# Re-forming the first token half of a fused attention and MLP kernel: two PSUM tiles for the second affine, row sums on ScalarE, a quarter of the value sort on GpSimd

## The chip, the core and the metric

The kernel runs on one core of a Trainium2 chip, from one launch. A core has five engines with a queue each: TensorE (PE in the profile, with its weight loads shown as PEld), VectorE (DVE), ScalarE (ACT), GpSimd (POOL) and SyncE (SP). Each works through its own instructions in the order of its queue, and they wait for each other by semaphores. The metric is the device time of one execution in microseconds (us); lower is better.

## The reference

Two stages, in float32, with batch 4, 8 heads, 768 positions, head size 64, 8 blocks of 96 positions, and a model width of 512:

```
P = sort_net                                  # (4, 8, 8, 8)
5 times: P = exp(P - max); P /= row sum; P /= column sum
k_sorted, v_sorted = P mixed over the 8 blocks of k and of v
attn = softmax(q_block . k_sorted_block^T / 8) . v_sorted_block   # inside a block of 96
x    = attn, heads side by side               # (4, 768, 512)
a1   = alpha1 * x + beta1
u    = x + lam * (w_tok @ a1)                 # w_tok is 768 x 768, over positions
a2   = alpha2 * u + beta2
out  = u + lam * (relu(a2 @ w_ch1) @ w_ch2)   # 512 -> 2048 -> 512
```

## The kernel before

The four batches run one after the other. The MLP of a batch is done in two halves of 384 positions. For a half, 16 hidden tiles of 128 units are made from the transposed input `a2T` (four matmuls of 128x384 each, `h_unit`; the page calls the output `h_ps`), and three tiles of 128 positions of output are made from them (16 matmuls of 128x512 each, `ch_unit`, `ch_ps`). All else, such as the attention of the next batch, the token product and the loads, is hung between these by the tables `put` and `run`: a key (batch, half, "h" or "c", number) says after which unit a piece is issued. There is no planner that moves an instruction. The class `Engine` keeps every instruction in the order in which the Python code issues it, so the order written by hand is the order of each queue. All compute instructions therefore show one source line, L65, and are told apart by their tiles.

Nothing can be hung between units before the first `a2T` of batch 0 exists. That head of the kernel, some 42 us, is what is touched here. Its steps are:

1. Five normalisations of `P` on VectorE and ScalarE, beside transposes of the queries on TensorE and `warm` matmuls on zeros, whose outputs nobody reads. The table `beside` holds what goes beside each.
2. `mix_keys` and `mix_values` spread `P` into the matrices `bigK` and `bigV`; `k_turn` and `k_copy` mix and transpose the keys of batch 0; `v_sort` re-orders the loaded values `v8` into `VD` (four instructions of 16 head columns: 128 partitions x 768 elements of float16, read with a stride of 64 elements), and `v_mix` makes the sorted values `Vs` from it, eight columns at a time. `score` gives the softmax numerators `et`, one group of heads and one half of the blocks per call.
3. `pv_first(g)` gives the attention output `x` for two heads (128 columns), in positions that are permuted so that all 128 partitions are used. `permute` copies `w_tok` into the same order (`wp`), `prep_wtok` transposes it on TensorE and copies it into `w_tokT`. "Half" 0 is the first 384 rows of `w_tok`.
4. The first token half. The columns of `u` come transposed straight from TensorE. For each of four groups of 128 columns, `first_tok` makes the token product in one PSUM tile (`tok_ps`, six matmuls), and begins a second tile (`turn_ps`) with the transposed `x` and a rank-one term, row sums of `w_tok` times `beta1 * lam`. ScalarE scales the product by `lam * alpha1` into `tok16`, and `first_turn` adds that to the second tile by a matmul with the identity. ScalarE's `affine` then reads the second tile and writes `a2T`. The row sums themselves are six matmuls against a column of ones (`row_sums`, `rr_ps`), and the per-column parameters are transposed by `prep_ab2`.

What sets the order around the change, in words of the code: lines 748 to 808 are the hand-written order of steps 2 to 4; lines 880 to 888 start the hidden tiles of the first half, with the last `first_turn` between them; lines 824 to 834 hang the second half of `w_tok` (`prep_wtok(ks, 1, ...)`), the rest of `a1` and the first output sums (`first_back`) between the first hidden tiles. PSUM tiles come from two pools: `psa` with two tiles of two banks, `psb` with four tiles of one bank. A tile is handed out again, in turn, once its last reader is done. GpSimd's queue issues the large loads (line 115 on, 149 to 155, 169 to 173, 299, 810); such an issue waits when the load that last used the same semaphore has not landed. The values `v8` are the third load.

```
    v_sort(0, act.copy)
    v_sort(1, copy)
    score(0, 0, 0, psa)
...
    for ci in range(2):
        for m in range(3):
            h_part(0, 0, m, [ci])
    first_turn(3, t3, act)
```

Of the kernel before, what the change touches and what calls it, by code (L numbers as in the profile page):

```python
# [7 lines left out]
FT = mybir.dt.float32  # L8
F16 = mybir.dt.float16
BF = mybir.dt.bfloat16  # L10
AF = mybir.ActivationFunctionType
ALU = mybir.AluOpType
# [4 lines left out]
def kernel(  # L17
# [25 lines left out]
    C = H * D  # L43
# [45 lines left out]
    def psb(shape, dtype, name):  # L89
        return pools["psB"].tile(shape, dtype, name=name, tag="psB")  # L90

    def const(shape, dtype, name):
        return wts.tile(shape, dtype, name=name, tag=name)
# [54 lines left out]
    for half in range(2):  # L148
# [7 lines left out]
        if half == 0:  # L156
# [2 lines left out]
                KT0[:].rearrange("p g i (th t) -> p (g i th) t", th=2)[:, :, HB:64].bitcast(FT), 0.0  # L159
            )  # L160

    W1p = const([128, CT, HID], BF, "W1p")
    W2p = const([128, HT, C], BF, "W2p")
    w1v = moe_w_ch1.rearrange("(ci p) n -> p ci n", p=128)
# [4 lines left out]
    pool.dma_start(alphaB[:], moe_alpha1.partition_broadcast(128))  # L169
    pool.dma_start(betaB[:], moe_beta1.partition_broadcast(128))  # L170
    pool.dma_start(lamB[:], moe_lam.partition_broadcast(128))
    for g in range(4):
        pool.dma_start(W1p[:, :, g * 512:(g + 1) * 512], w1v[:, :, g * 512:(g + 1) * 512])
    brow = att.tile([1, C], F16, name="brow", tag="uT", bufs=2)
    rrow = att.tile([1, 384], F16, name="rrow", tag="uT", bufs=2)
    ones16 = const([128, 1], F16, "ones16")
    pool.memset(ones16[:], 1.0)
    pool.tensor_tensor(brow[:], bet1[:], lam1[:], ALU.mult)

    vscr = dram.tile([B, H * NB, BLK, D], F16, name="vscr", tag="vscr")  # L180
# [41 lines left out]
    def warm(n, ps=psa):  # L222
        fill(ps([128, 512], FT, "warm_ps")[:], n)
# [27 lines left out]
            ps[half].rearrange("p (t r) -> p r t", t=6),  # L251
        )

    def v_sort(n, eng):
        eng(
            VD[:, n * 16:(n + 1) * 16, 0:HB],
            v8[:, :, n * 16:(n + 1) * 16].rearrange("p t d -> p d t"),
        )

    rsum = const([BH, NB], FT, "rsum")  # L260
    csum = const([BH, NB], FT, "csum")
# [6 lines left out]
    def q_out(g):  # L268
        for half in range(2):
            q_copy(0, g, qps[g], half, act.copy)  # L270
# [3 lines left out]
        1: [lambda: q_first(1), lambda: warm(2), lambda: warm(3)],  # L274
        2: [lambda: q_first(2), lambda: warm(3)],
        3: [lambda: q_out(0), lambda: q_first(3)],
        4: [lambda: q_out(1), lambda: q_out(2), lambda: q_out(3), lambda: warm(5)],
    }
    warm(12)
    for it in range(5):  # L280
# [89 lines left out]
    def k_turn(b, g, ps):  # L370
        return turn_slab(k8, lambda r, g: bigK[b][r, g, :], g, "k_ps", ps)
# [61 lines left out]
    def pv_first(g):  # L433
        if g == 0:
            x_of[0] = moep.tile([128, 8, C], F16, name="x128", tag="x128", bufs=2)
            a1_of[0] = moep.tile([128, 8, C], F16, name="a1", tag="a1", bufs=1)
        ps = psa([128, 2, 512], FT, "x_ps")[:, :, 0:480].rearrange("p a (k d) -> p a k d", d=80)
        for i in range(NB):
            for h2 in range(2):
                et = ets[(0, g, i // 4)][:].rearrange("p a i t -> p (a i t)")  # L440
                lo = (4 * h2 + i % 4) * BLK
                w = min(128, 8 * BLK - lo)
                val = Vs[0][:, (2 * g + h2) * NB + i, 0:D + 1]
                if i < 6:
                    pe.matmul(ps[0:w, h2, i, 0:D + 1], et[:, lo:lo + w], val, start=True, stop=True)
                else:
                    for a in range(3):
                        pe.matmul(
                            ps[96:128, h2, 3 * (i - 6) + a, 0:D + 1], et[:, lo + a * 32:lo + (a + 1) * 32], val,
                            start=True, stop=True,  # L450
                        )
        rc = att.tile([128, 2, 6], FT, name="rc", tag="rc", bufs=3)
        dve.reciprocal(rc[:], ps[:, :, :, D])
        dve.tensor_tensor(
            x_of[0][:, 0:NT, g * 128:(g + 1) * 128].rearrange("p k (a d) -> p k a d", a=2),
            ps[:, :, :, 0:D].rearrange("p a k d -> p k a d"),
            rc[:].rearrange("p a k -> p k a").unsqueeze(3).to_broadcast([128, NT, 2, D]), ALU.mult,
        )
# [100 lines left out]
    w_tokT = const([128, NT, S], F16, "w_tokT")  # L559
    wp_of = {}  # L560

    def permute(half, eng):
        wp = wp_of[half] = (moep, att)[half].tile(
            [128, 3, NT, 128], F16, name="wp", tag=("u16", "raw")[half], bufs=(1, 2)[half]
        )
        src = wt16[half]
        eng(wp[:, :, :, 0:96], src[:, :, 0:TAIL].rearrange("p m (k c) -> p m k c", c=96))
        eng(wp[:, :, :, 96:128], src[:, :, TAIL:S].rearrange("p m (k c) -> p m k c", c=32))

    def prep_wtok(ks, half, ps, eng):  # L570
        pst = ps([128, 384], F16, "wtok_ps")
        for m in range(3):
            pe.transpose(pst[:, m * 128:(m + 1) * 128], wp_of[half][:, m, ks, :], ident16[:])
        eng(w_tokT[:, ks, half * 384:(half + 1) * 384], pst[:])

    ab2col = const([128, 4 * CT], FT, "ab2col")

    def prep_ab2(ps):
        tps = ps([128, 4 * CT], FT, "ab2_ps")
        pe.transpose(tps[:], ab2[:], ident16f[:])  # L580
        act.copy(ab2col[:], tps[:])
        dve.tensor_tensor(
            ab2col[:, 3 * CT:4 * CT], ab2col[:, 2 * CT:3 * CT], ab2col[:, 3 * CT:4 * CT], ALU.mult
        )

    def row_sums(ps):
        ps = ps([1, 384], FT, "rr_ps")
        for ks in range(NT):
            pe.matmul(ps[:], ones16[:], w_tokT[:, ks, 0:384], start=(ks == 0), stop=(ks == NT - 1))
        act.copy(rrow[:], ps[:])  # L590

    u_of = {}
# [5 lines left out]
    def affine(b, hf, ci, src, eng):  # L598
        dst = a2T_of[b][hf][:, ci, :]
        if eng is act:  # L600
            act.activation(
                dst, src, AF.Identity, bias=ab2col[:, CT + ci:CT + ci + 1], scale=ab2col[:, ci:ci + 1],
            )
        else:
            dve.tensor_scalar(
                dst, src, ab2col[:, ci:ci + 1], ab2col[:, CT + ci:CT + ci + 1], op0=ALU.mult, op1=ALU.add,
            )
# [5 lines left out]
            u_of[b] += [t_[:, kt, :] for kt in range(3)]  # L613
        a2T_of[b] = [moep.tile([128, CT, 384], BF, name=f"a2T_{hf}", tag="a2T", bufs=3) for hf in range(2)]

    def first_tok(g):
        c = slice(g * 128, (g + 1) * 128)
        tps, ups = (psb([128, 384], FT, n)[:] for n in ("tok_ps", "turn_ps"))
        for ks in range(NT):
            pe.matmul(  # L620
                tps, x_of[0][:, ks, c], w_tokT[:, ks, 0:384], start=(ks == 0), stop=(ks == NT - 1),
            )
        for m in range(3):
            pe.matmul(
                ups[:, m * 128:(m + 1) * 128], x_of[0][:, m, c], ident16[:],
                start=(m == 0), stop=True, skip_group_check=True,
            )
        pe.matmul(ups, brow[:, c], rrow[:], start=False, stop=True, skip_group_check=True)
        act.activation(tok16[:, g, :], tps, AF.Copy, scale=ab2col[:, 3 * CT + g:3 * CT + g + 1])
        return ups  # L630

    def first_turn(g, ups, eng):
        pe.matmul(ups, ident16[:], tok16[:, g, :], start=False, stop=True, skip_group_check=True)
        affine(0, 0, g, ups, eng)

    def first_back(m, ps):
        ps = ps([128, C], FT, "back_ps")
# [107 lines left out]
    def wtok(ks, eng):  # L745
        prep_wtok(ks, 0, psb, eng)

    mix_keys(0, psb)
    warm(4)
    kp0 = k_turn(0, 0, psb)  # L750
    kp1 = k_turn(0, 1, psb)
    k_copy(0, 0, kp0, 0, copy)
    k_copy(0, 0, kp0, 1, act.copy)
    warm(1)
    kp2 = k_turn(0, 2, psb)
    k_copy(0, 1, kp1, 0, copy)
    k_copy(0, 1, kp1, 1, act.copy)
    kp3 = k_turn(0, 3, psb)
    k_copy(0, 2, kp2, 0, copy)
    k_copy(0, 2, kp2, 1, act.copy)  # L760
    mix_values(0, psb)
    k_copy(0, 3, kp3, 0, copy)
    k_copy(0, 3, kp3, 1, act.copy)
    v_sort(0, act.copy)
    v_sort(1, copy)
    score(0, 0, 0, psa)
    score(0, 0, 1, psa)
    warm(3, psb)
    v_mix(0, 0, psb, copy)
    v_mix(0, 1, psb, copy)  # L770
    v_sort(2, copy)
    score(0, 1, 0, psa)
    v_mix(0, 2, psb, copy)
    v_mix(0, 3, psb, act.copy)
    v_sort(3, act.copy)
    score(0, 1, 1, psa)
    v_mix(0, 4, psb, copy)
    v_mix(0, 5, psb, copy)
# [2 lines left out]
    v_mix(0, 7, psb, copy)  # L781
    dve.tensor_copy(Vs[0][:, :, D:GRP], mgap[:].unsqueeze(2).to_broadcast([128, H * NB, GRP - D]))
    score(0, 2, 1, psa)
    permute(0, copy)
    moe_start(0)
    warm(1, psb)
    pv_first(0)
    wtok(0, act.copy)
    wtok(1, act.copy)
    wtok(2, act.copy)  # L790
    score(0, 3, 0, psa)
    pv_first(1)
    wtok(3, act.copy)
    wtok(4, act.copy)
    wtok(5, act.copy)
    score(0, 3, 1, psa)
    permute(1, copy)
    row_sums(psb)
    prep_ab2(psb)
    t0 = first_tok(0)  # L800
    pv_first(2)
    first_turn(0, t0, act)
    t1 = first_tok(1)
    pv_first(3)
    first_turn(1, t1, act)
    t2 = first_tok(2)
    first_turn(2, t2, act)
    t3 = first_tok(3)

    load_kv(1)  # L810
    load_q(1)
# [5 lines left out]
    def put(b, hf, kind, n, *todo):  # L817
        at.setdefault((b, hf, kind, n), []).extend(todo)
# [5 lines left out]
    for kt in range(3, NT):  # L824
        put(0, 0, "h", 4 + kt, lambda kt=kt: moe_tok(0, kt, psb))
    for ks in range(NT):
        put(0, 0, "h", ks, lambda ks=ks: prep_wtok(ks, 1, psb, (dve.tensor_copy, act.copy)[ks % 2]))
    for n in range(1, B):
        put(max(n - 2, 0), n > 1, *(("h", 10), ("c", 9))[n > 1], lambda n=n: mix_matrix(n))
    put(0, 0, "h", 9, lambda: moe_cross(0, 1))  # L830
# [46 lines left out]
        put(b, 0, "h", 4, lambda b=b: moe_cross(b, 1))  # L877
        put(b, 0, "h", 13, lambda b=b: moe_affine(b, 1))

    for ci in range(2):  # L880
        for m in range(3):
            h_part(0, 0, m, [ci])
    first_turn(3, t3, act)
    for m in range(3):
        h_part(0, 0, m, [2])
    for m in range(3):
        h_part(0, 0, m, [3])
        run(0, 0, "h", m)
# [41 lines left out]
```

## Time and profile before

| What | Value |
|---|---|
| Median of 9 runs | 274.42 us (272.89 to 275.54) |
| Profiled execution, its own time | 276.2 us |
| Its span, from first to last instruction | 274.4 us |
| Mean granted TensorE clock | 0.994 of full speed |
| Busy: PE, DVE, ACT, POOL | 95%, 62%, 43%, 35% of the span |
| First hidden matmul that completes a tile | starts at 41.90 us |

The page's first part gives the busy time of each engine. The second cuts the span in 40 slices of 6.9 us and shows tenths of busy time in each. The chain of waits follows the last instruction back to whatever released it, step by step, and so shows the work that set the end; each line is a start, a length and a piece of work, "x6" being six instructions. A timeline lists one engine's instructions with the idle time before them, and a table of groups gives the mean length of one instruction. In the profile a matmul's length includes its latency; the distance from one start to the next is what a row of matmuls costs.

### The profile page before, as it was taken

The numbers are of one execution on the slowest core, as the hardware profiler recorded it, in microseconds if no ns is written. First come the engines' busy times: TensorE is split into PE (matmuls) and PEld (weight loads), VectorE is DVE, ScalarE is ACT, GpSimd is POOL, SyncE is SP. The second block draws the span as 40 slices with busy tenths as digits, with TensorE's granted clock in tenths as the row PEclk, the third lists the DMA queues.
The fourth block names the chain that finished last, engine by engine and source line by source line (L and its number), as shares of the span: only waits on it lengthen the run. The fifth ranks groups of instructions, "written<-read, shape, count | busy, mean of one in ns | idle before, by whom it ended". The sixth has DMA issues, their size and how long they took to land.

```text
span 274.4 us, 5380 instructions
## 1 busy us (share of the span) xinstructions
PE 261.3 (95%) x2173; PEld 140.5 (51%) x2173; DVE 169.8 (62%) x351; ACT 117.1 (43%) x219; POOL 96.4 (35%) x104
## 2 busy tenths in 40 slices
PE   7888999999999999999999969999999999999993
PEld 3455655455556444554565424554465445545552
DVE  5778427896558978576778725586689756121032
ACT  2578648234787002453674002444674004604600
POOL 8647202701472094403570814402300746122000
PEclk9999999999999999999999997999999999999999
DMA  6999999997989942249399942149300223012012
GB/s 100 194 205 201 206 208 214 174 122 178 128 168 174 141 116 78 59 115 155 79 188 161 113 124 67 38 118 118 102 13 2 73 61 76 22 38 76 0 41 76
DMA packets 67372, 31.04 MB, mean 113 GB/s; under 512 B 56642, under 2 KB 63058, under 8 KB 67348
## 3 DMA queue, kind: packets, MB, share of 16 engines
q0 software_dynamic: 26352, 15.34, 40.4%
q1 hardware_dynamic: 40900, 15.30, 30.6%
q8 instruction: 17, 0.28, 0.4%
q14 instruction: 7, 0.06, 0.1%
q10 hardware_dynamic: 96, 0.07, 0.1%
HBM read 32.79 MB, written 8.65 MB: 151 GB/s over the span
## 4 chain that ended last, share of the span: by engine, by line
PE 85%; DVE 5%; DMA 4%; issue 2%; ACT 1%; SPq 1%; POOL 0%; DVEq 0%; POOLq 0%
PE h_ps L65 30%; PE ch_ps L65 28%; PE tok_ps L65 12%; PE x_ps L65 3%; DMA q<-in_q_dram 3%; PE sc_ps L65 3%; DVE ost L65 2%; PE kmix_ps L65 1%; PE mix_ps L65 1%; PE warm_ps L65 1%; DVE x L65 1%; DVE a L65 1%; SPq L670 1%; PE turn_ps L65 1%; PE v_ps L65 1%
## 5 line engine op out<-in xcount | busy, mean ns | idle before, releaser
L65 PE MATMUL h_ps<-a2T,W1p 128*128 128x384 bf16 x512 | 96.8, 327 | 2.7 <-DVE a2T L65 2.4
L65 ACT ACTIVATE hTa<-h_ps 128x384 bf16<-128x384 f32 x96 | 47.0, 492 | 95.5 <-PE h_ps L65 95.3
L65 PE MATMUL ch_ps<-W2p,hTa 128*128 128x512 bf16 (+1 forms) x300 | 68.5, 371 | 0.0
L65 POOL TENSOR_TENSOR ost<-ost,u 128x512 f32<-128x512 f32 x21 | 26.6, 1266 | 116.5 <-DVE ost L65 110.4
L65 PEld LDWEIGHTS <-W1p 128*128 128x128 bf16 x512 | 47.5, 99 | 35.2 <-issue 4.8
L65 PEld LDWEIGHTS <-hTa 128*128 128x128 bf16 x300 | 28.4, 98 | 29.0
L65 DVE TENSOR_TENSOR ost<-ch_ps,lamB 128x512 f32<-128x512 f32 (+1 forms) x25 | 16.7, 669 | 37.8 <-PE ch_ps L65 34.6
L65 POOL TENSOR_TENSOR u<-toktmp,x 128x512 f32<-128x512 f32 x18 | 29.2, 1635 | 6.7 <-DVE toktmp L65 6.7
L65 PE MATMUL tok_ps<-a,w_tokT 128*128 128x512 f16 x126 | 31.0, 391 | 0.0
L65 ACT ACTIVATE et<-sc_ps 96x768 f16<-96x768 f32 (+1 forms) x32 | 25.6, 812 | 10.9 <-PE sc_ps L65 10.9
L65 PE MATMUL ch_ps<-W2p,hTb 128*128 128x512 bf16 (+1 forms) x100 | 24.8, 370 | 0.0
L65 DVE TENSOR_TENSOR toktmp<-tok_ps,lamB 128x512 f32<-128x512 f32 x21 | 14.4, 687 | 11.9 <-PE tok_ps L65 10.5
L65 PEld LDWEIGHTS <-w_tokT 128*128 128x128 f16 x126 | 12.5, 100 | 14.9 <-issue 1.7
L65 DVE TENSOR_TENSOR u<-toktmp,x 128x512 f16<-128x512 f32 (+1 forms) x24 | 18.9, 799 | 0.7
L65 ACT ACTIVATE hTb<-h_ps 128x384 bf16<-128x384 f32 x32 | 15.7, 490 | 8.0 <-PE h_ps L65 7.6
L65 POOL DMA_DIRECT2D qn<-in_q_dram x18 | 16.0, 924 | 4.6 <-DMA raw<-in_v_dram 4.6
L65 DVE CAST kT<-kmix_ps 64x512 f16<-64x512 f32 x20 | 14.3, 713 | 4.5 <-PE kmix_ps L65 3.0
L65 DVE TENSOR_TENSOR x<-x_ps,rcb 96x512 f16<-96x512 f32 x24 | 16.5, 687 | 0.8
L65 DVE TENSOR_SCALAR a2T<-uT,ab2col 128x384 bf16<-128x384 f16 x28 | 10.5, 440 | 9.5 <-DMA uT<-u 9.5
L65 PE MATMUL x_ps<-Vs,et 96*128 96x65 f16 (+4 forms) x288 | 14.4, 195 | 1.4 <-DVE x L65 1.0
L65 PEld LDWEIGHTS <-et 96*128 96x128 f16 (+4 forms) x288 | 12.4, 100 | 6.3 <-DVE x L65 2.2
L65 ACT CAST kT<-kmix_ps 64x512 f16<-64x512 f32 x16 | 11.5, 716 | 9.8 <-PE kmix_ps L65 9.6
(113 smaller groups left out, 238.1 us busy)
## 6 DMA issues: line engine op xcount, KB each, us to landing
out_dram<-ost SPq DMA_DIRECT2D x23, 192.0 KB, 2.2
raw<-in_v_dram POOLq DMA_DIRECT2D x6, 384.0 KB, 8.0
raw<-in_k_dram POOLq DMA_DIRECT2D x6, 384.0 KB, 10.0
qn<-in_q_dram POOLq DMA_DIRECT2D x18, 128.0 KB, 10.2
vscr<-mixed SPq DMA_DIRECT2D x6, 384.0 KB, 3.6
Vs<-vscr SPq DMA_DIRECT2D x3, 768.0 KB, 7.7
W1p<-in_moe_w_ch_dram POOLq DMA_DIRECT2D x4, 512.0 KB, 13.1
W2p<-in_moe_w_ch_dram POOLq DMA_DIRECT2D x4, 512.0 KB, 17.3
```

The costliest lines, as they stand in the source:

```text
L65: ins = getattr(self.eng, name)(*args, **kwargs)
L670: nc.sync.dma_start_transpose(uT[:, :, m * 128:(m + 1) * 128], u16_of[b][:, 3 * hf + m, :],)
```

## The change

- `first_mm` and `first_turn` replace `first_tok` and the old `first_turn`. The token product stays in its own PSUM tile. The second tile holds the transposed `x` and the rank-one term; ScalarE applies scale and bias to it and writes `z` in float32. VectorE's `first_finish` then forms `a2T = product * (alpha2 * lam * alpha1) + z`. The four matmuls with the identity that added `tok16` are gone; ScalarE still writes `tok16`, which `first_back` needs. `ab2col` gets four more columns for the new factor (`prep_scales`).
- `row_sums`: ScalarE passes over `w_tok` three times with `accum_out` (`row_sum(m)`, output thrown into the still unused tile `a1`), and three small transposes on TensorE turn the sums into a row.
- `v_sort(3)` runs on GpSimd, ahead of the loads of `W1p`; `v_sort(0)` goes from ScalarE to VectorE and `v_sort(2)` from VectorE to ScalarE.
- `mix_values`, `prep_ab2` and `prep_scales` are issued earlier, `permute(0)` is cut in two parts, five of the six `prep_wtok` copies of half 0 go from ScalarE to VectorE, `pv_first(2)` is issued ahead of the token products, the last group's transposes and product (`first_turn(3)`, `first_mm(3)`) stand between the hidden matmuls of `ci` 0 and 1, and the `prep_wtok` of half 1 takes its PSUM tiles from `psa` instead of `psb`.

```diff
+    v_sort(3, pool.tensor_copy)
     for g in range(4):
         pool.dma_start(W1p[:, :, g * 512:(g + 1) * 512], w1v[:, :, g * 512:(g + 1) * 512])
...
-    ones16 = const([128, 1], F16, "ones16")
-    pool.memset(ones16[:], 1.0)
...
+    def row_sum(m):
+        if m == 0:
+            a1_of[0] = moep.tile([128, 8, C], F16, name="a1", tag="a1", bufs=1)
+        act.activation(a1_of[0][:].rearrange("p k c -> p (k c)")[:, 0:S], wt16[0][:, m, :], AF.Copy, accum_out=rcol[:, m:m + 1])
...
     def row_sums(ps):
-        ps = ps([1, 384], FT, "rr_ps")
-        for ks in range(NT):
-            pe.matmul(ps[:], ones16[:], w_tokT[:, ks, 0:384], start=(ks == 0), stop=(ks == NT - 1))
+        rc16 = const([128, 3], F16, "rc16")
+        act.copy(rc16[:], rcol[:])
+        ps = ps([1, 384], F16, "rr_ps")
+        for m in range(3):
+            pe.transpose(ps[:, m * 128:(m + 1) * 128], rc16[:, m:m + 1], ident16[:])
         act.copy(rrow[:], ps[:])
...
+    def first_finish(g):
+        dve.scalar_tensor_tensor(
+            a2T_of[0][0][:, g, :], tps_of[g], ab2col[:, 4 * CT + g:4 * CT + g + 1], z_of[0][:, g, :],
+            op0=ALU.mult, op1=ALU.add,
+        )
+        if g == 3:
+            tok_copy(g)
...
-    def first_turn(g, ups, eng):
-        pe.matmul(ups, ident16[:], tok16[:, g, :], start=False, stop=True, skip_group_check=True)
-        affine(0, 0, g, ups, eng)
...
+        if g == 0:
+            z_of[0] = moep.tile([128, CT, 384], FT, name="z", tag="u32", bufs=3)
+        act.activation(
+            z_of[0][:, g, :], ups, AF.Identity, bias=ab2col[:, CT + g:CT + g + 1], scale=ab2col[:, g:g + 1],
+        )
+        if g < 3:
+            first_finish(g)
...
     mix_keys(0, psb)
     warm(4)
+    mix_values(0, psb)
+    prep_scales()
...
-    mix_values(0, psb)
+    v_sort(0, copy)
+    score(0, 0, 0, psa)
     k_copy(0, 3, kp3, 0, copy)
     k_copy(0, 3, kp3, 1, act.copy)
-    v_sort(0, act.copy)
+    score(0, 0, 1, psa)
     v_sort(1, copy)
...
-    v_sort(2, copy)
+    v_sort(2, act.copy)
...
-    permute(0, copy)
+    row_sum(0)
+    permute(0, copy, 0, 3)
...
-    wtok(0, act.copy)
+    score(0, 3, 0, psa)
+    wtok(0, copy)
     wtok(1, act.copy)
-    wtok(2, act.copy)
-    score(0, 3, 0, psa)
+    wtok(2, copy)
+    permute(0, copy, 3, 6)
+    row_sum(1)
+    row_sum(2)
     pv_first(1)
-    wtok(3, act.copy)
-    wtok(4, act.copy)
-    wtok(5, act.copy)
+    wtok(3, copy)
+    wtok(4, copy)
+    wtok(5, copy)
+    permute(1, copy, 0, 6)
     score(0, 3, 1, psa)
-    permute(1, copy)
+    pv_first(2)
     row_sums(psb)
-    prep_ab2(psb)
-    t0 = first_tok(0)
-    pv_first(2)
-    first_turn(0, t0, act)
-    t1 = first_tok(1)
+    first_mm(0, psb)
+    first_turn(0, psb)
+    first_mm(1, psb)
     pv_first(3)
-    first_turn(1, t1, act)
-    t2 = first_tok(2)
-    first_turn(2, t2, act)
-    t3 = first_tok(3)
+    first_turn(1, psb)
+    first_mm(2, psb)
+    first_turn(2, psa)
...
-        put(0, 0, "h", ks, lambda ks=ks: prep_wtok(ks, 1, psb, (dve.tensor_copy, act.copy)[ks % 2]))
+        put(0, 0, "h", ks, lambda ks=ks: prep_wtok(ks, 1, psa, (dve.tensor_copy, act.copy)[ks % 2]))
...
-    for ci in range(2):
+    for m in range(3):
+        h_part(0, 0, m, [0])
+    first_turn(3, psa)
+    first_mm(3, psa)
+    for ci in (1, 2):
         for m in range(3):
             h_part(0, 0, m, [ci])
-    first_turn(3, t3, act)
-    for m in range(3):
-        h_part(0, 0, m, [2])
```

## The prediction

> **What bounds the kernel now.** First the page: who is busy, and is the clock granted?
>
> ```profile
> PE 261.3 (95%) x2173; PEld 140.5 (51%) x2173; DVE 169.8 (62%) x351; ACT 117.1 (43%) x219; POOL 96.4 (35%) x104
> ...
> PE   7888999999999999999999969999999999999993
> ...
> PEclk9999999999999999999999997999999999999999
> ```
>
> TensorE is full except in the first four slices (0 to 27 us) and in slice 24. So after the head an engine other than TensorE costs nothing unless it makes TensorE wait, and time taken out of the head reaches the end. Next the chain of waits, cut to the head:
>
> ```profile
> 17.42 1.53 ACT vd L65
> ...
> 25.15 1.33 DVE wp L65 x2
> ...
> 29.94 1.06 PE rr_ps L65 x6
> 31.01 0.16 PE ab_ps L65
> ...
> 33.63 0.27 PE turn_ps L65
> ...
> 36.26 0.27 PE turn_ps L65
> ...
> 37.54 0.59 ACT tok L65
> 38.13 0.04 issue
> 38.17 0.32 PE turn_ps L65
> ...
> 40.98 0.18 PE turn_ps L65
> 41.16 0.02 issue
> 41.18 0.68 ACT a2T L65
> 41.86 0.04 issue
> 41.90 0.34 PE h_ps L65
> ```
>
> Up to 25 us the head alternates between TensorE and copies of the value sort. From 30 us it is TensorE's own list, in which the row sums, the parameter transpose, the four adding matmuls and two waits on ScalarE stand.
>
> **Token stage (before: 29.9 to 41.9 us).** Row sums: 1.06 us leave; three transposes come, 0.06 us apart as the `wtok_ps` ones are, with latency 0.2. Gain 0.85. The parameter transpose (0.16) goes to 11 us in the place of one warm matmul (0.21 from start to start): gain 0.15, no cost. The four adding matmuls cost from start to start 0.17, 0.17, 0.57 (0.40 of it the wait for `tok` at 38.1) and 0.16; after the fourth, TensorE stands 0.43 for `a2T` (next matmul due at 41.47, start 41.90). Together 1.5. In the new order the last `a2T` needs the fourth product, which lies six hidden matmuls (6 x 0.163 = 1.0) ahead of its first reader: latency 0.2 and one VectorE instruction. That one has no row. Nearest is `toktmp` (PSUM and SBUF in, 512 elements, 0.69), so 0.55 for 384; bounds 0.45 and 0.7. It fits either way. `z` on ScalarE costs what `a2T` did there (0.67). I count 1.4 of the 1.5, for the transposes' own latencies.
>
> **Middle (25.2 to 31.1 us).** `pv_first(2)` (0.96) moves ahead of the products, so it is neither gain nor loss. VectorE takes five `wtok` copies (0.35 each, 1.8), ScalarE loses five of 0.48 and gets three row sums. No row has an accumulator; a float16 copy of 384 takes 0.48 and an exponential of 768 takes 0.83: I take 0.85, bounds 0.8 and 1.2. At 0.85 they end at 29.4, before the last scores need ScalarE at 29.8; at 1.2 the chain of row sum, transpose and `rrow` copy is late for the first rank-one matmul by 0.3. VectorE now paces this stretch: normalising `x`, 1.22 each for four; `permute` in pieces, 0.6 and 0.3 twice, then 1.4; the copies. Laid end to end, TensorE waits some 0.6 in place of today's 0.3 at 26.2 and the time of the row sums: the stretch from the first `x_ps` to the first product stays 5.9 to 6.0 us although 1.0 us of TensorE work left and 0.96 came. Cost 0.1.
>
> **First stretch (12 to 25.2 us).** `mix_values` now stands before the keys: three VectorE instructions of 0.22 and two of 0.16 come ahead of the first key copy, which ends at 15.8, not 15.24; the third key turn waits for that PSUM tile. The scores start at 17.3, not 17.08. The 0.5 us of "issue" inside the key turns I leave in place. Then the values, which landed at 17.22. Quarter 0 on VectorE: 17.3 to 18.1 (on ScalarE it ended at 18.94). Quarter 1 follows a key copy, 18.45 to 19.25 if nothing blocks it. Quarter 2 on ScalarE ends at 20.95, behind two exponentials; quarter 3 is GpSimd's.
>
> The price of that one: GpSimd's only copy row (256 elements, 0.42) gives 1.25 for 768; the same strided read takes ScalarE 1.51 against 0.83 unstrided, so up to 2.5. [...] I take 1.9; alone it would be done long before it is read (22.8), and costs nothing.
>
> [...] Here VectorE and GpSimd collide:
>
> ```profile
> 64.35 1.62 DVE L65 TENSOR_SCALAR a2T<-uT,ab2col 128x384 bf16<-128x384 f16 x2
> ```
> ```profile
> 64.30 1.27 POOL L65 TENSOR_TENSOR ost<-ost,u 128x512 f32<-128x512 f32 x1 [11.27 <-DVE ost L65]
> ```
> ```profile
> L65 PE MATMUL h_ps<-a2T,W1p x9: 326/326/337, 72.8 to 74.9; 128*128 128x384 bf16 x9
> L65 DVE TENSOR_SCALAR a2T<-uT,ab2col x4: 366/368/1330, 64.1 to 65.9; 128x384 bf16<-128x384 f16 x4
> ```
>
> Three of the four take 0.37; the one that began just after GpSimd's instruction took 1.33 and ended 0.1 after it. Instructions of VectorE that read PSUM show no such growth. [...] So I expect the lock. [...]
>
> The two sums for the first `x_ps`, before 25.21. Without the lock: `v_mix` 4 waits for quarter 2 (20.95), the 0.5 us "issue" gap, the last copies of `Vs` end at 24.2, `x_ps` at 24.35: gain 0.85. With it: `v_mix` 2 at 20.65, 4 at 21.8, gap, last copy 25.05, `x_ps` at 25.1: gain 0.1.
>
> GpSimd's sort also holds back the first `W1p` issue from 17.5 to 20.1. Five earlier loads are still under way then (they land up to 26.7), the queue doesn't run dry at its 205 GB/s, and `W1p` lands at 29, needed at 36.5.
>
> **The sum.** With the lock: 0.1 + 0.85 + 0.15 + 1.4 - 0.1 = 2.4 us: the first completing hidden matmul goes from 41.90 to 39.5. The `prep_wtok` change takes away a 0.25 wait of TensorE for `hTa`, yet gains nothing: VectorE's row of two copies and four `a1` pairs (42.43 to 47.56) ends when the next token product (47.35) reads it, and two `psa` tiles make TensorE wait on it earlier. That row starts 2.4 sooner too. Then TensorE is full, and the shift stays. What doesn't move is the load queue: at 205 GB/s the last queries of batch 1 land at 59.5 now and then. They are read at 64.4, afterwards 62.0: still hidden, and uncovered only past a gain of 4.9. The `uT` transposes come at 54.0 instead of 56.4, more under those loads; their reader on VectorE has no TensorE work behind it until 70. The profiled execution took 276.2, 1.8 more than its span and 1.8 above the median, so I subtract from the median: 274.42 - 2.4 = **272.0 us**.
>
> **The rivals.**
> - No lock, or a sort of 1.2 us: x_ps at 24.35, the gain is 3.1 to 3.2: 271.3. [...]
> - VectorE becomes the bound of the middle: its list from 25 to 32 us holds some 7 us of work. If row sums cost 1.2, or the pieces of `permute` and the copies wait for each other twice more, 1.1 of the gain is lost: 273.1. For it: idle TensorE at 26.2 already waits for `wp`. Against: ScalarE's load does not grow.
> - Slower, by the clock. TensorE's wait for the third `v_mix` is some 1.4 us (19.2 to 20.65) at a sort of 1.9. In slice 24 TensorE stood 2.39 us, and then ran 3.2 us at half clock:
>
> ```profile
> 165.50:168.70 3.20, 3.20 (x10) 1.22 (x9) 1.85 (x7) 0.49 (x1) 1.26 (x1) 0.50 0.00 0
> ```
> A sort of 3.6 us makes the wait 3.1: 1.7 more for the wait and 1.7 for the half clock, so +1.0: 275.4. It decides from a sort of about 3.1 us, 4 ns per element, where the copy row has 1.6.
> - The gain is given back after 60 us (queries, or `uT` landing late): 274.4. Against it, the slacks above.
>
> **How the numbers follow.** Lock as summed 0.45 (own range 271.2 to 272.9), no lock 0.25, VectorE-bound 0.15, slower 0.10, given back 0.05. 0.3% (0.8 us) is what a measurement of this kernel can tell from no change. Below 273.6 lie the first two and two thirds of the third: faster 0.80; slower 0.11; same 0.09. The range reaches from the no-lock case with the cheap row sums (270.6) over the VectorE case to 274.3; outside lie the slower case and small ends of the others.
>
> **What would show it.** `rr_ps` with three short transposes; no `turn_ps` matmul that reads `tok`; the first completing hidden matmul near 39.5. The lock: a `vd` copy on VectorE of about 2 us that ends with GpSimd's, and `x_ps` from 25.1; without it two of 0.8 and 24.35. The VectorE case: `x_ps` and `wtok_ps` released by DVE with over 1 us of wait in all. The prediction is wrong if TensorE shows new waits past 40 us, if the first product starts after 31.5, or if the clock row shows half speed in the head.

## The result, and the profile after

The changed kernel takes 271.75 us (median of 16 runs, 271.02 to 273.66); the kernel before, run beside it, 274.42 (51 runs, 272.83 to 276.73). The ratio is 0.991, with a 95% interval of 0.989 to 0.993. The forecast was 272.0, and faster. The number is right. Only part of the way to it is. Executions with a mean granted clock below 0.995 (32 of 99 of the kernel before, 7 of 40 of the changed kernel and its repeats, over the sets that list the clock) are about 2 us longer, and the ratios leave the longest of them out; without them the medians are 273.99 and 271.73, so most of the gain does not come from them.

The profiled execution took 272.24 us, its span is 270.4. First the page's busy times and slices:

```profile
PE 257.4 (95%) x2165; PEld 138.8 (51%) x2165; DVE 174.6 (65%) x363; ACT 116.4 (43%) x220; POOL 98.6 (36%) x104
...
PE   7988899999999999999999979999999999999993
...
PEclk9999999999999999999999999999999999999999
```

Two places differ. The head (slices 1 to 4) is filled differently, not obviously better. Slice 24 still has a dent, but a 7 instead of a 6, and the clock row no longer has a 7 behind it. The chain of waits, cut to the head:

```profile
16.00 0.47 DVE kT L65
16.46 0.05 issue
16.51 2.12 DVE vd L65
...
21.73 0.90 issue
...
25.30 1.03 PE x_ps L65 x24
...
28.45 0.65 issue
...
31.75 0.03 PE rr_ps L65
31.78 0.03 PE x_ps L65
31.81 0.08 PE rr_ps L65 x2
31.89 1.08 PE tok_ps L65 x6
32.97 0.43 PE turn_ps L65 x4
33.40 1.08 PE tok_ps L65 x6
...
39.48 1.14 PE h_ps L65 x7
```

From 31.75 us on all is as meant: the row sums are three transposes between the last `x_ps` products, no `turn_ps` matmul waits for `tok`, ScalarE is not on the chain. The seventh of the `h_ps` row, the first that completes a tile, starts at 40.30 us (the row starts at 39.32 and goes on every 0.163); before it was 41.90. So the shift at that point is 1.6 us, not the 2.4 of the forecast. Ahead of it stand a `vd` copy of 2.12 us on VectorE, which took 0.8 before, and two pauses of 0.90 and 0.65 us that nothing releases ("issue").

At slice 24 the shift is 1.5 us (161.97 and 160.47 us). The other 2.5 us between the two profiles (274.4 - 270.4 - 1.5) come there, where TensorE stands until VectorE has the second affine of the third sequence. The waits of TensorE from 155 to 165 us, before and after:

```profile
PE h_ps L65 <- DVE a2T L65: 2.4, 1, 2.4
```
```profile
PE h_ps L65 <- DVE a2T L65: 1.6, 1, 1.6
```

That is 0.8 us. The last 1.7 us are the 3.4 us at half clock that followed this wait in the profile of before (shown ahead of the result) and don't follow it here.

### The profile page after: what moved, and what is told of

The parts are those of the page before. It is cut to its first block, busy times and chain, and to the rows that moved or that the text cites. A ratio compares the mean times of both kernels' runs of the same rounds, so it can differ in the third digit from the quotient of the medians.

```text
span 270.4 us, 5381 instructions
## 1 busy us (share of the span) xinstructions
PE 257.4 (95%) x2165; PEld 138.8 (51%) x2165; DVE 174.6 (65%) x363; ACT 116.4 (43%) x220; POOL 98.6 (36%) x104
## 4 chain that ended last, share of the span: by engine, by line
PE 79%; DVE 12%; DMA 4%; issue 3%; SPq 1%; DVEq 0%; POOLq 0%
PE h_ps L65 29%; PE ch_ps L65 24%; PE tok_ps L65 10%; DVE a L65 4%; PE x_ps L65 4%; DVE x L65 3%; PE sc_ps L65 2%; PE warm_ps L65 2%; DVE ost L65 2%; DMA uT<-u 2%; DMA q<-in_q_dram 2%; PE kmix_ps L65 1%; PE v_ps L65 1%; PE mix_ps L65 1%; DVE vd L65 1%
## 5 line engine op out<-in xcount | busy, mean ns | idle before, releaser
L65 PE MATMUL tok_ps<-a,w_tokT 128*128 128x512 f16 x126 | 29.7, 379 | 0.1
L65 DVE TENSOR_TENSOR u<-toktmp,x 128x512 f16<-128x512 f32 (+1 forms) x24 | 19.5, 825 | 0.7
L65 PEld LDWEIGHTS <-w_tokT 128*128 128x128 f16 x126 | 12.2, 98 | 14.3 <-issue 0.6
L65 DVE CAST kT<-kmix_ps 64x512 f16<-64x512 f32 x20 | 14.2, 709 | 4.5 <-PE kmix_ps L65 3.0
```

The source lines that it names most:

```text
L65: ins = getattr(self.eng, name)(*args, **kwargs)
```

## Experiments

All are compared with the kernel before, run beside them on the same chip. The columns are read from each profile: the start of the first `tok_ps` product of batch 0; from there to the first `tok_ps` product of the second token half; TensorE's wait in front of the third sequence; then the median of all runs and the ratio.

| Kernel | First tok_ps, us | To second half, us | Wait, us | Median, us | Ratio to before (95%) |
|---|---|---|---|---|---|
| before | 31.10 | 16.25 | 2.39 | 274.4 | |
| after | 31.82 | 13.93 | 1.61 | 271.75 | 0.991 (0.989 to 0.993) |
| a_again | 30.73 | 13.93 | 1.78 | 271.85 | 0.992 (0.989 to 0.995) |
| b_head | 31.63 | 16.25 | 2.59 | 275.67 | 1.003 (1.000 to 1.007) |
| b_token | 30.39 | 13.93 | 1.54 | 273.52 | 0.994 (0.990 to 0.997) |
| a_rows_old | 32.80 | 13.93 | 2.44 | 273.09 | 0.997 (0.994 to 1.001) |
| a_add_back | 31.25 | 15.99 | 1.78 | 274.89 | 1.003 (0.999 to 1.006) |
| a_sort_act | 31.20 | 13.92 | 1.77 | 271.56 | 0.989 (0.986 to 0.993) |
| a_shift | 35.04 | 13.93 | 2.16 | 275.93 | 1.001 (0.996 to 1.006) |
| b_fill | 30.34 | 16.25 | 1.01 and fill | 274.45 | 0.999 (0.996 to 1.002) |
| a_fill | 30.99 | 13.93 | 0.67 and fill | 273.08 | 0.994 (0.991 to 0.997) |
| a_out_late | 31.78 | 13.93 | 1.44 | 271.89 | 0.992 (0.989 to 0.995) |
| b_token_late | 30.47 | 13.93 | 1.67 | 272.56 | 0.993 (0.989 to 0.996) |
| a_best | 30.98 | 13.92 | 0.69 | 270.81 | 0.987 (0.983 to 0.991) |

**1. Which half carries it.** `b_head` has only the first stretch of the change, `b_token` everything but it.

```diff
# b_head: the kernel before, and
+    v_sort(3, pool.tensor_copy)          # ahead of the W1p loads
...
+    mix_values(0, psb)                   # ahead of the keys
...
+    v_sort(0, copy)                      # was act.copy; v_sort(2) the other way round
+    score(0, 0, 0, psa)                  # between the key copies
# b_token: the kernel after, and
-    (these)
```

> The kernel before with only the first stretch of the change (mix_values early, the v sorts dealt out to VectorE, ScalarE and GpSimd, the scores between the key copies, other warm counts); the token stage stays as before. [...] Rival, the prediction's sum without a lock: 0.85 us less (0.997). By the prediction's sum with the lock: 0.1 us less.

> The change without its first stretch: the order and the v sorts up to the last score of the third group as before, everything of the token stage as after. Theory from the two traces: the token stage carries the whole gain in the head, 1.5 to 2.4 us, and with what the later stall of TensorE gives back or takes the time is 271.0 to 272.9 (ratio 0.988 to 0.995). Rival, the two parts work only together (the middle is paced by VectorE, which the earlier sorts had relieved): under 1 us gained (over 0.996).

`b_head` came out at 1.003, a little above the 1.000 to 1.002 (0 to 0.5 us more) that the author expected from the two traces and not as the forecast's sums did, though its interval reaches down to no change; `b_token` at 0.994, near the upper end of its range. The column "To second half" says it almost without scatter. The way from the first token product to the second half is 16.25 us with the old token stage and 13.93 with the new one, whatever stands ahead. The column "First tok_ps" says what the first stretch costs in the head. With the old one the first token product is at 31.10, 30.34, 30.39 and 30.47 us (before, b_fill, b_token, b_token_late); with the new one, in the five kernels that leave the rest ahead of it alone (after, a_again, a_out_late, a_fill, a_add_back), at 31.82, 30.73, 31.78, 30.99 and 31.25. The means are 30.58 and 31.31, so about 0.7 us are lost, although the two sets overlap. The single profile of before, 31.10, was one of the late ones, which hid this. At the end of the kernel the loss does not show: `b_token` and its repeat take 273.52 and 272.56 us, no less than the changed kernel. Seven and five of their twelve times have a clock below 0.995, and a later wait takes back some of it (see the rivals below).

**2. Two terms of the sum.** `a_rows_old` takes the row sums back, `a_add_back` the adding matmuls.

```diff
# a_rows_old
-    row_sum(0) ... row_sum(2)            # ScalarE's running sums
...
-            pe.transpose(ps[:, m * 128:(m + 1) * 128], rc16[:, m:m + 1], ident16[:])
+            pe.matmul(ps[:], ones16[:], w_tokT[:, ks, 0:384], start=(ks == 0), stop=(ks == NT - 1))
# a_add_back
-            first_finish(g)              # VectorE: product * factor + z
+            pe.matmul(ups_of[g], ident16[:], tok16[:, g, :], start=False, stop=True, skip_group_check=True)
+            affine(0, 0, g, ups_of[g], act)
```

> The changed kernel with the row sums of w_tok made by the six products with a column of ones again, instead of ScalarE's running sums and three transposes. Theory (the prediction's term): the token stage, from the first x_ps product to the first tok_ps product of the second half, is 0.6 to 0.85 us longer, the time about 0.8 us above the changed kernel (ratio to before 0.993 to 0.995). Rival (ScalarE's three passes of 1.0 us hold up something in the middle, so that most of the saving was already spent): under 0.3 us.

> The changed kernel with the four adding matmuls back: the token product goes through tok16 and a 128x384 matmul onto the turned x, and ScalarE makes the affine; the order stays that of the changed kernel. Theory (the prediction's term of 1.4 us): the same stretch is 1.0 to 1.8 us longer, the time 1.0 to 1.8 us above the changed kernel (ratio to before 0.994 to 0.998). Rival (the products of the next group hide the matmuls, only their own 0.16 us each count): 0.6 to 0.8 us.

Row sums: the way from the first `x_ps` to the first `tok_ps` product, less the pause in it, is 31.82 - 25.30 - 0.65 = 5.87 us in the changed kernel (5.86 in a_again) and 32.80 - 25.25 - 0.91 = 6.64 with the old sums: 0.77 us. Adding matmuls: the way to the second half grows from 13.93 to 15.99: 2.06 us, more than the range. In the timeline of TensorE their waits can be read beside them:

```profile
33.07 0.32 PE L65 MATMUL turn_ps<-tok,ident 128*128 128x384 f16 x1 [0.24 <-ACT tok L65]
...
37.66 0.32 PE L65 MATMUL turn_ps<-tok,ident 128*128 128x384 f16 x1 [0.24 <-ACT tok L65]
...
40.65 0.32 PE L65 MATMUL turn_ps<-tok,ident 128*128 128x384 f16 x1 [0.67 <-ACT tok L65]
```

Put back into the new order, they wait at three places (0.24, 0.24, 0.67), for each comes right behind its own product. In the old order they had cost less: the change took 16.25 - 13.93 = 2.32 us out of this way, of which 0.96 is `pv_first(2)`, moved ahead of it, so 1.36 is the matmuls and their waits. The medians rise by 1.3 and 3.1 us, more than 0.77 and 2.06. In the profile of `a_add_back` another 1.09 us goes to a wait of TensorE for `a2T` at 104 us; experiment 5 shows where a further part comes from.

**3. The lock.** What VectorE and GpSimd did with the value sort in the changed kernel (timelines: start, length, instruction, count, and in brackets the idle time ahead of it):

```profile
16.00 0.56 DVE L65 CAST kT<-k_ps 128x384 f16<-128x384 f32 x1 [0.19 <-PE k_ps L65]
16.51 2.11 DVE L65 COPY vd<-v 128x768 f16<-128x768 f16 x1
18.54 0.55 DVE L65 CAST kT<-k_ps 128x384 f16<-128x384 f32 x1
19.01 0.82 DVE L65 COPY vd<-v 128x768 f16<-128x768 f16 x1
```
```profile
16.47 1.47 POOL L65 COPY vd<-v 128x768 f16<-128x768 f16 x1 [1.78 <-DMA v<-in_v_dram]
17.88 3.00 POOL L65 DMA_DIRECT2D W1p<-in_moe_w_ch_dram  x3
```

GpSimd began 0.04 us ahead of VectorE and held it up: VectorE's copy ends at 18.62 us, 0.68 after GpSimd's. This is what the prediction calls the lock. `a_sort_act` gives GpSimd's quarter to ScalarE.

```diff
-    v_sort(3, pool.tensor_copy)
     for g in range(4):
         pool.dma_start(W1p[:, :, g * 512:(g + 1) * 512], w1v[:, :, g * 512:(g + 1) * 512])
...
     v_mix(0, 3, psb, act.copy)
+    v_sort(3, act.copy)
```

> The changed kernel with the third quarter of the v sort given back from GpSimd to ScalarE, in its old place. Theory (the copies on VectorE and GpSimd shut each other out, which costs VectorE's first sort 1.3 us and TensorE's first v_ps product 0.5 us): VectorE's first sort takes 0.8 instead of 2.1 us, the wait in front of the first v_ps product falls from 1.1 to about 0.5 us, the first x_ps product comes 0.2 to 0.6 us sooner than in the unaltered changed kernel, and so does the end (ratio to before 0.987 to 0.991). Rival (ScalarE with two quarters is late, or an instruction-load pause takes the gain): no gain, 0.991 to 0.993.

```profile
16.60 0.83 DVE L65 COPY vd<-v 128x768 f16<-128x768 f16 x1
17.35 0.55 DVE L65 CAST kT<-k_ps 128x384 f16<-128x384 f32 x1
17.81 0.82 DVE L65 COPY vd<-v 128x768 f16<-128x768 f16 x1
```

So the lock is shown: without GpSimd's copy beside it the first sort takes 0.83 us instead of 2.11 (1.97 in `a_again`, 1.84 in `b_head`), and TensorE's first `v_ps` product starts at 17.65 instead of 18.68 us, with no wait. But the first `x_ps` product starts at 24.82 us, within what the changed kernel shows (24.44 to 25.30). The 1.0 us is gone by then, and the timeline of TensorE says where (`a_sort_act`, then `a_again`):

```profile
20.20 0.40 PE L65 MATMUL v_ps<-bigV,vd 64*64 64x64 f16 x13
21.78 0.47 PE L65 MATMUL v_ps<-bigV,vd 64*64 64x64 f16 x19 [1.18 <-issue]
```
```profile
21.82 0.47 PE L65 MATMUL v_ps<-bigV,vd 64*64 64x64 f16 x19 [0.16 <-issue]
```

The pause took it: it is 1.18 us long here and 0.16 in `a_again`, and ends at the same time. (In after it ends at 22.63 us; experiment 4 comes to that.) The clock also stood at half from 22.8 to 26.2 us in this profile, but that cost little: in `a_best`, which has the same head and ran it at full clock, the first `x_ps` product starts at 24.70 us, after 0.54 us of waiting for `Vs`. So giving the quarter back does not undo the 0.7 us that the first stretch loses (first token product at 31.20 and 30.98 us), and what causes that loss was not isolated. The time, 0.989, is 0.3 us under that of a_again, and the intervals overlap: a gain of the order of 0.3 us is likely, not shown.

**4. What the pauses are.** The page leaves them without a cause. The kernel before has two of half a microsecond (and a longer step of 0.18 us in front of its 480th matmul):

```profile
16.67 0.34 PE L65 MATMUL k_ps<-bigK,k 64*64 64x64 f16 x10 [0.53 <-issue]
22.59 0.47 PE L65 MATMUL v_ps<-bigV,vd 64*64 64x64 f16 x17 [0.52 <-issue]
```

The trace lists packets of a queue of kind "instruction", 16,384 bytes each; one starts 2.2 to 2.4 us ahead of the end of each pause in before and after. The pauses lie exactly 128 matmuls apart, in front of the 224th and 352nd in before, the 350th and 478th in after. That one packet brings TensorE the instructions of 128 matmuls, a block, is the author's estimate from that distance. `a_shift` puts 36 matmuls more ahead of everything, at no more columns.

```diff
-    warm(12)                             # 12 of 512 columns
+    fill_n(48)                           # 48 of 128 columns, same zeros
```

> The changed kernel with its first 12 warm matmuls of 512 columns cut into 48 of 128, so 36 matmuls more ahead of all the rest and no more columns. Theory (the pauses of TensorE with no releaser, in front of the 350th and 478th matmul of the trace, are its instructions arriving from memory, one page of 128 matmuls at a time): the pauses stay in front of about the 350th and 478th matmul counted from the start, which are now pieces of work 36 matmuls earlier; the time moves by less than 0.5 us. Rival (the pauses belong to the work, a register step or a buffer at that place): they stay at the same pieces of work, now about the 386th and 514th matmul.

TensorE's instructions counted from the span's start to just before the end of each pause (stretch, its length, busy time and count, clock, DMA share, GB/s); the changed kernel, then `a_shift`:

```profile
0.00:22.60 22.60, 18.66 (x349) 1.00 0.97 170
...
0.00:29.05 29.05, 23.98 (x477) 1.00 1.02 179
```
```profile
0.00:21.10 21.10, 18.45 (x349) 1.00 0.96 173
0.00:28.10 28.10, 22.89 (x477) 0.99 1.02 177
```

The pauses stay in front of the 350th and 478th matmul, now 36 matmuls earlier in the work. They belong to the count, not to the work, which is what a block of instructions that is late would do. The second has grown:

```profile
24.89 0.99 PE L65 MATMUL x_ps<-Vs,et 128*128 128x65 f16 x23 [0.33 <-DVE Vs L65]
28.14 0.22 PE L65 MATMUL x_ps<-Vs,et 128*32 128x65 f16 x1 [2.26 <-issue]
```

It ends at 28.14 us, and where it shows in the profiles with the new token stage it ends at 27.6 to 29.3 us. That time is not fixed, it moves with the start of the block before. In all 14 profiles the load of the block that begins with the 478th matmul (480th in kernels with the old token stage) starts 3.7 to 4.8 us after TensorE has begun the block before it, and that matmul starts 2.2 to 2.7 us after the load does. So this block takes 5.9 to 7.0 us, however early TensorE is through with it. What was saved inside a block made the pause at its end longer (1.18 us in `a_sort_act`, 0.16 in `a_again`); what brought TensorE sooner to the start of a block was kept: the 350th matmul starts at 22.63 us in after and at 21.82 in `a_again`, the 478th at 29.10 and 28.01. Why one execution of the same kernel gets its block 0.8 us sooner than another was not found. The time expected, under 0.5 us of change, was missed by the median of 275.93 us: after the long pause this profile ran 6.8 us at half clock, and it is one of five of the twelve executions with a mean clock of 0.981, which took 276.8 to 277.8 us.

**5. The wait at 160 us.** Two theories: that the change made a half clock there rarer, tested by filling the wait with seven warm matmuls in both kernels, and that the chain that TensorE waits for is one on SyncE's queue.

```diff
+    put(1, 1, "c", 11, lambda: warm(7, psb))     # b_fill, a_fill
```

> The kernel before with seven more warm matmuls of 512 columns put behind the last output group of the second sequence, where TensorE stands idle for 2.4 us in its trace and then runs at half clock for 3.4 us. Theory (part of the gain of the change is that this half clock comes less often): no half clock behind the stall, the median 0.5 to 1.7 us lower than before (ratio 0.994 to 0.998), and the lowest times unchanged. Rival (the half clock is rare in the runs, the gain is all in the head): the same time within 0.3 us.

> The changed kernel with the same seven warm matmuls at the same place (idle for 1.6 us in its trace, no half clock behind it). Theory: nothing to win, 0 to 0.2 us beside the changed kernel (ratio to the kernel before 0.990 to 0.992), and the highest times, which showed a lower granted clock, gone. Rival (the half clock plays no part): the same ratio with the same scatter.

None of the 12 times of `b_fill` shows a low clock, and yet the median didn't move; `a_fill` is worse than the changed kernel by more than was expected. The theory's sizes are missed. A part is plain in the profiles: with the fill the way from the first hidden matmul of the third sequence to the end of the span is 108.75 us (both), without it 108.4, so behind the wait the fill costs 0.35. In the profile of `a_fill` TensorE also waits 0.45 us at 101 us, where that of after does not.

Then the queue. SyncE's own timeline, before and after:

```profile
157.01 0.53 SPq L737 DMA_DIRECT2D out_dram<-ost  x1
157.60 1.29 SPq L738 DMA_DIRECT2D out_dram<-ost  x1
158.98 3.82 SPq L670 DMA_TRANSPOSE uT<-u  x3
```
```profile
155.47 0.53 SPq L777 DMA_DIRECT2D out_dram<-ost  x1
156.05 0.42 SPq L778 DMA_DIRECT2D out_dram<-ost  x1
156.56 3.83 SPq L710 DMA_TRANSPOSE uT<-u  x3
```

The queue works without a gap: six transposes of queries, two output transfers, three transposes `uT`, and these set TensorE's wait. In before one issue takes 1.29 instead of 0.42 us, and this excess of 0.87 us is about the 0.8 by which TensorE waits longer. At 157.60 us a 16 KB instruction load starts as well. In the changed kernel no load lies between 155 and 161 us; it comes at 163.11. Three more runs repeat the changed kernel and try to take the two output transfers out of the chain.

```diff
# a_again: the kernel after, unaltered
# a_out_late, b_token_late: the pair of transfers kept back at its old place, and
...
+    put(1, 1, "c", 4, out_late)                  # issued behind moe_cross
```

> The changed kernel once more, unaltered, as the mark for the next three and for a second look at its trace. Expected: 271.5 to 272.3 us (ratio 0.989 to 0.993). The place where TensorE waits for the second affine of the third sequence: theory A (the stall is 1.6 us plus what an instruction load that meets the sync engine's transfers adds) expects 1.6 us where no 16 KB instruction load lies on the chain of the uT transposes and 2.2 to 2.8 us where one does; theory B (the change itself shortened the stall by 0.8) expects 1.6 us again in either case. First x_ps product at 24.4 to 25.3 us.

> The changed kernel with one pair of output transfers (second sequence, fourth row group) issued behind the three uT transposes on the sync engine's queue instead of ahead of them. Theory (TensorE's wait at 160.5 to 162.1 us is the end of a chain on the sync engine in which these two issues take 1.05 us, and up to 1 us more where an instruction load meets them): the wait falls from 1.6 to about 0.55 us (1.1 to 1.7 with a load), the time by 1.0 us against the unaltered changed kernel (ratio 0.986 to 0.989), and the long times with a low granted clock are gone. Rival (the transposes then wait for VectorE's u instead): under 0.3 us gained.

> The change without its first stretch, with the same pair of transfers moved behind the transposes: the candidate that should beat both. Theory: against the earlier run of the change without its first stretch (0.9935) 1.0 us less for the transfers and up to 0.6 us for the half clock that came in seven of its twelve times: 270.5 to 271.5 us (ratio 0.985 to 0.989). Rival (the half clock comes for another reason than a long wait of TensorE): again over half of the times with a clock of 0.994 or lower, ratio 0.990 or more.

In `a_out_late` and `b_token_late` the pair stayed ahead of the transposes: the order by hand holds the compute engines' queues, but not SyncE's transfers. So both are repeats of the changed kernel and of `b_token`, and say nothing on the transfers. As repeats they are of use. `a_again` and `a_out_late` have no load on the chain and wait 1.78 and 1.44 us; both theories expected about that.

Over all 14 profiles, before and after included, an instruction load starts between 154.3 and 159.4 us in nine, and in each of them the SyncE issue beside it takes 0.56 to 1.22 us longer; in the other five (after, a_again, a_out_late, a_sort_act, a_best) it starts at 162.1 to 163.4 us, past the chain and 1.0 to 1.6 us after TensorE goes on, and no issue is lengthened. Repeats of one kernel agree in this, so the place seems to follow the program. The load alone does not set the wait, though, and theory A as it was put is not met: `b_token`, `b_token_late` and `a_add_back` have a load on the chain and wait only 1.54, 1.67 and 1.78 us. There the six transposes start 14.2 to 14.3 us before TensorE comes to the wait, in the other kernels without the fill 13.1 to 13.5 us, and the chain, 0.8 to 1.2 us longer, has that much more time. That the load causes the longer issue is a coincidence found nine times, not an experiment; why these five programs load later was not found.

`a_best` holds the order on SyncE as well, on top of `a_sort_act`:

```diff
+            if (b, hf) == (2, 0):
+                tc.keep_in_program_order(ins)            # the uT transposes
...
+        tc.keep_in_program_order(act_out(out[1, 3 * 96:4 * 96, :], ost[0:96, :]))
+        tc.keep_in_program_order(act_out(out[1, TAIL + 3 * 32:TAIL + 4 * 32, :], ost[96:128, :]))
```

> The candidate: the changed kernel with the sort quarter on ScalarE instead of GpSimd, and the pair of output transfers that the two earlier runs were to move now really behind the three uT transposes in the sync engine's queue (held there in program order). Theory: the stall of TensorE at about 160 us falls from 1.6 or 1.8 to about 0.6 us, and the times are 1.0 us below those with the sort quarter alone (0.989): 270.3 to 271.0 us, ratio 0.985 to 0.987. Rival (the transposes then wait for VectorE, or the transfers meet the next stage): under 0.3 us, ratio 0.988 to 0.990.

```profile
146.62 8.21 SPq L516 DMA_TRANSPOSE qT<-qn  x6
154.93 3.84 SPq L709 DMA_TRANSPOSE uT<-u  x3
158.86 0.53 SPq L747 DMA_DIRECT2D out_dram<-ost  x1
```
```profile
160.53 1.19 PE L65 MATMUL h_ps<-a2T,W1p 128*128 128x384 bf16 x4 [0.69 <-DVE a2T L65]
```

The wait falls to 0.69 us, the median to 270.81 us (6 runs, 270.13 to 271.06), the ratio to 0.987 (0.983 to 0.991). It is the lowest of all, and clear of the kernel before; it is 0.9 us under the changed kernel and 0.75 under `a_sort_act` by the medians, with overlapping intervals of the ratios. That the chain on SyncE is what TensorE waited for is shown by the wait itself.

## Why the prediction was right, and where it was not

- **Token stage: right, with its sizes.** Row sums 0.85 forecast, 0.77 measured; adding matmuls and their waits 1.4, measured 1.36. The middle, forecast at 5.9 to 6.0 us from the first `x_ps` to the first product, is 5.87 without the pause. The parameter transpose (0.15) wasn't measured alone. VectorE's new instruction took 0.62 us instead of 0.55 and hides as was said; a row sum took 0.85, but ScalarE then issues a separate instruction of 0.19 that reads the sum, unforeseen and hidden too:

```profile
28.03 0.86 ACT L65 ACTIVATE a<-wt 128x768 f16<-128x768 f16 x1
28.77 0.20 ACT L65 ACTIVATION_READ_ACCUMULATOR a<-wt 128x1 f32 x1
```

- **First stretch: the lock right, the sum wrong.** The lock came, but GpSimd was first and VectorE's quarter 0 was blocked, not quarter 1 (the values landed at 16.4 us, in before at 17.2). No run shows the 1.9 us for GpSimd's copy from which the sum with the lock is worked out: it took 1.47 us in after. TensorE's wait for a sorted quarter came in front of the first `v_ps` product (1.08 us), not of the third `v_mix`. Why VectorE's copy waits for GpSimd's, no run shows. The step "first `x_ps` at 25.1, gain 0.1" was nearly met by the two profiles (25.21, then 25.30), but that of before was a late one: the old first stretch shows 24.11 to 24.46 in three other profiles. The gain of 0.1 is a loss of about 0.7 at the first token product, 0.4 of it already there at the first `x_ps`, by the means; the rest is the pause at the 478th matmul.
- **"The 0.5 us of 'issue' inside the key turns I leave in place", and the "gap" of 0.5 us in both sums for the first `x_ps`: the step that failed.** Pauses that nothing releases were taken as fixed lengths that move along with the work. The one inside the key turns (0.53 us in before) is in none of the other 13 profiles. The one among the `v_mix` products measured 0.90 us in after, 0.16 in its repeat and 1.18 in `a_sort_act`, and behind it came one of 0.65 us in after that no sum holds. By experiment 4 each ends when the next block of instructions is there, 2.2 to 2.5 us after its load has started, and what the work inside the block gained came out of it. The first rival, no lock and 271.3, leant on the same assumption; `a_sort_act` shows it: 1.0 us gained on `a_again` at the first `v_ps` product, nothing of it left at the end of the pause.
- **"Then TensorE is full, and the shift stays": incomplete.** The shift does stay, 1.6 us at the first completing hidden matmul and 1.5 at 160 us. But the sum looked for what the change could lose behind the head and not for what could be gained there. The wait in slice 24 is 0.8 us shorter, and an issue on SyncE's chain takes 0.42 us instead of 1.29; the instruction load that lay beside it at 157.60 us comes later, at 163.11. That is 0.8 us that no step of the forecast holds.
- **The sum.** By the profiles the second token half starts at 46.97 us with the old order (mean of before and b_fill) and at 45.26 with the new one (after, a_again, a_out_late, a_fill): 1.7. With 0.8 at the wait it is 2.5 us; the forecast had 2.4, 2.3 of it from the token stage alone. A loss of 0.7 and a gain of 0.8, both unforeseen, nearly cancel. That the time met the forecast to 0.3 us is to that extent luck; what the forecast had right is the token stage.
- **Its own signs of being wrong.** One of them came: the first product starts at 31.82 us in after, past the 31.5 that was set (31.78 and 30.73 in the repeats), for the pauses are longer. The first completing hidden matmul was to be near 39.5 us and starts at 40.30.
- **Rivals.** Half clock in the head was not seen in the changed kernel's three profiles, but `a_sort_act` and `a_shift` show that it lies near: there 3.4 and 6.8 us at half clock came with pauses of 1.18 and 2.26 us, and in the first GpSimd sorted nothing. "Given back after 60 us" shows in `b_token`, which is 0.9 us earlier than the changed kernel at the second half (44.32 and 44.40 against a mean of 45.26) and then waits 1.13 us for `a2T` at 100 us (0.96 in its repeat); SyncE had waited for the queries' landing there until 85.8 us. The same wait is in the profiles of `a_add_back` (1.09), `a_sort_act` (0.90), `a_fill` (0.45) and `a_best` (0.36), and not in those of the changed kernel and its repeats. `a_add_back` comes to the second half at 47.24 us, later than all of these, so being early does not explain it; its cause stays open.

## What to carry to other kernels

An idle stretch that no releaser explains is to be read by its count. Here it stood in front of the 350th and 478th matmul also with 36 matmuls more ahead of the work (`a_shift`), its end 2.2 to 2.5 us after the start of an instruction load, and the 1.0 us saved inside the block ahead of it was not kept (`a_sort_act`). Whether fewer instructions help there, no run tried. Terms read from start-to-start distances of one engine's own list, as in the token stage here, came out to a tenth of a microsecond (0.85 against 0.77, 1.4 against 1.36); a stage in which several engines and loads meet needs more than one profile of the kernel before anything is subtracted from it. And a stall far behind the change deserves a look at the queue that ends it: here the wait at 160 us fell from 1.77 us in `a_sort_act` to 0.69 in `a_best`.

## What the runs showed of the hardware

- The pauses of TensorE that nothing releases stand 128 matmuls apart, and in before and after a packet of 16,384 bytes starts on the queue of kind "instruction" 2.2 to 2.4 us ahead of the end of each. At the 350th and 478th matmul of this head (352nd and 480th with the old token stage) the load of a block starts 3.3 to 4.8 us after the block before it has begun, and a pause, where there is one, ends 2.2 to 2.5 us later; pauses of up to 2.3 us stand there. If a packet holds a block, as the author estimates, TensorE was then through with a block of small matmuls before the next one was there.
- A transfer issue on SyncE beside a 16 KB instruction load took 0.56 to 1.22 us longer in nine profiles of nine at this place. They were seen together, not taken apart.
- A wait of 1.78 us of TensorE at this place was once followed by 3.4 us at half clock, and once, 1.77 us long in `a_sort_act`, was not; one of 2.44 us in `a_rows_old` was, one of 2.59 us in `b_head` was not. So the length alone does not decide. The first, in `a_again` (the wait, then the stretch behind it; the last three numbers are clock, DMA share, GB/s):

```profile
159.38:161.16 1.78, 0.00 (x0) 1.00 0.68 156
162.10:165.50 3.40, 3.40 (x10) 0.50 0.03 5
```

The half-clock stretches measured behind waits and pauses were 3.4 us long (`a_again`, `a_sort_act` and before) or twice that, 6.8 us (`a_shift`). What decides whether one follows was not found.
